# Second mixture weights loaded piece by piece into the tiles of first ones, with the dense part's first columns behind four first weights

## The chip, the cores and the metric

The kernel runs on one core of a Trainium2 chip. The time is the device time of one execution in microseconds (us). Before the change it is 387.07 us, the median of three runs (386.13 to 389.33).

## The reference, cut to what matters

Three stages follow each other, all in 32-bit floats except the last stage's weights, which are 64-bit floats in HBM.

1. Attention over 4 batches, 8 heads, 576 positions and 64 dimensions, with a local mask in four heads and a strided one in the other four. Its output, laid out as x of 2304 x 512, goes on.
2. A soft mixture of 8 experts. `logits = x @ phi` gives 32 slots, 4 for each expert. The softmax over tokens, transposed, times x gives the slot inputs. For each expert e, `h = max(slot_input[e] @ w1[e], 0)` and `slot_out[e] = h @ w2[e]`, where w1[e] is 512 x 1024 and w2[e] is 1024 x 512, 2 MB each. The softmax over slots times slot_out gives the new x.
3. A dense part: `h = x @ w_in` (512 x 2048), an ELU, and `g @ w_out` (2048 x 512) into the 2304 x 512 output.

## The kernel before, in words

Everything is emitted in one function. All DMAs are issued by SyncE (SP in the profile), in program order; its program lets eight transfers be under way, so a ninth waits until the one eight places ahead has landed. Each engine takes its instructions in order.

The attention runs over "units"; during them SP loads q, k and v and then the first mixture weights w1[0] to w1[7], as the table `LOADS` says, each into a "slot": a region of SBUF that q, k, v or a mask used before. `slot(i, name)` allocates a new tile in the region, and a new tile waits until every access to the tile before it in that region is done. `load_w(e, second, s)` loads weight w1[e] or w2[e] into slot s, in four transfers of 512 KB, w1 by halves of its rows and columns (line 459), w2 by two of its eight blocks of 128 rows (line 462). w2[0] and w2[1] go into the two halves `wb0` and `wb1` of the tile `xw`; w2[2], w2[3], w2[4], w2[5], w2[6] and w2[7] go into the slots of w1[0], w1[1], w1[2], w1[4], w1[6] and w1[7].

`emit_w1(a)` multiplies the slot inputs by w1 of experts 2a and 2a + 1 (line 638): for each of the four blocks of rows c, four matmuls side by side in four column groups of the array. `emit_h1T` transposes the result. `emit_w2(e)` (line 729) multiplies by the eight blocks of w2[e]; all eight experts add into one PSUM tile `yp` (called acc in the profile). Behind each pair of blocks of the last expert, and behind `emit_w2`, stand warm-up matmuls on the identity (`warm`, line 419; others, line 1088, stand where the dense part begins).

The dense weights come as 64-bit floats and are decoded: `dec_abs` on ScalarE (line 708), then `dec_1`, `dec_2`, `dec_3` on VectorE (lines 712, 716, 722). The first 256 columns of w_in (`WP`) are loaded by themselves, 1 MB in one transfer into slot 9, by `load_w64(0, 0, 9, (0, WP))` (line 697), ahead of w2[7]; the decoded values go over w2[0] in `wb0`. Behind the last expert SP loads pieces of w_out (line 703, 512 KB each) into `wb1` and the other 256 columns of the first part of w_in (line 697).

After the mixture `y_sb`, `sop` and `soT` turn yp into the operand of the dense part (lines 777 to 784). `soT` times the decoded w_in (`mps`, lines 860 to 877) gives a small matrix `M4`; from there the units of the dense part run: `hps` (line 951), the ELU (lines 955 to 971) and three output matmuls for each 128 tokens (lines 993 to 995). Their order is written by a planner with fixed costs and due times, which the change does not touch.

Of the kernel before, what the change touches and what calls it, by code (L numbers as in the profile page):

```python
# [10 lines left out]
I32 = mybir.dt.int32  # L11
# [8 lines left out]
def attn_moe_mlp(ctx, tc, q, k, v_l, v_s, phi, w1, w2, w_in, w_out, out):  # L20
    nc = tc.nc
    B, S, D = 4, q.shape[1] * q.shape[3] // 4, 64
    NT, DM = out.shape
    NE, _, FE = w1.shape
    w_in, w_out = w_in.bitcast(I32), w_out.bitcast(I32)
# [30 lines left out]
    WP, HP = 256, 2  # L56
# [14 lines left out]
    def region(tag, name):  # L71
        return slots.tile([128, SIZE[tag]], F32, tag=tag, name=name)

    def slot(i, name):
        if not isinstance(i, int):
            return i
        t = region(SLOT_AT[i], name)
        return t[:, 0:min(SLOT, t.shape[1])]
# [276 lines left out]
    with tc.manual_schedule():  # L355
# [7 lines left out]
        for b in range(B):  # L363
            sm_ = smask[32 * b:32 * b + 32, 0, :]
            nc.gpsimd.affine_select(
                out=sm_, in_=sm_, compare_op=ALU.is_ge, fill=NEG, base=0,
# [3 lines left out]
        for e in range(2):  # L370
            nc.vector.memset(qk_t[2][1][:, e, 0:576], 0.0)
        nc.vector.tensor_copy(
            out=smask16.rearrange("p (a b) -> p a b", b=MR), in_=smask.to_broadcast([128, 16, MR])
# [14 lines left out]
        for b in range(B):  # L388
            lm = lmask[32 * b:32 * b + 32]
            nc.gpsimd.affine_select(  # L390
                out=lm[:, 0:32], in_=lm[:, 0:32], compare_op=ALU.is_ge, fill=NEG, base=0,
# [3 lines left out]
                out=lm[:, 32:64], in_=lm[:, 32:64], compare_op=ALU.is_ge, fill=NEG, base=-1,  # L395
# [29 lines left out]
        for x in (576, 1152):  # L425
            for e in range(2):
                w = x // 576 * 576
                nc.scalar.activation(
                    out=qk_t[2][1][:, e, x:x + w], in_=zero.to_broadcast([128, w]), func=AF.Copy,
                )  # L430
        for b in range(B):
            nc.scalar.activation(
                out=e0[32 * b:32 * b + 32].rearrange("p (g x) -> p g x", x=32),
                in_=ident[0:32, 0:32].unsqueeze(1).to_broadcast([32, B, 32]), func=AF.Copy,
# [10 lines left out]
            load_k(3, c, c + 2)  # L445
            load_v_str(3, c // 2)

        wsl = {}

        def load_w(e, second, s, part=None):  # L450
            if (e, second) not in wsl:
                t = slot(s, f"w{e}_{second}")[:, 0:4096]
                wsl[e, second] = t.rearrange("p (c x) -> p c x", c=8 if second else 4)
            t = wsl[e, second]
            src = (w2 if second else w1)[e].rearrange("(c p) x -> p c x", p=128)
            if not second:
                for c in (0, 2):
                    for x in (0, 512):
                        nc.sync.dma_start(out=t[:, c:c + 2, x:x + 512], in_=src[:, c:c + 2, x:x + 512])
                return  # L460
            for c in range(0, 8, 2) if part is None else range(part, part + 4, 2):
                nc.sync.dma_start(out=t[:, c:c + 2], in_=src[:, c:c + 2])
# [103 lines left out]
        emit_dt(0)  # L566
        emit_PV(nu - 1, s_ps)
        load_w(7, 0, 1)
        emit_L(*pend_L.pop())
        emit_m(1)  # L570
# [37 lines left out]
        for t in range(3):  # L608
            nc.vector.tensor_scalar(
                out=e1[:, t], in0=e0[:, 0:NS], scalar1=rd, scalar2=wt[:, t:t + 1], op0=ALU.mult, op1=ALU.mult  # L610
# [19 lines left out]
        for t in (misc.tile([128, 1024], F32, tag="pst", name="h1T"), small("xt", 768, "h1T_b", 1), small("s", 256, "h1T_c", 3)):  # L630
            nc.gpsimd.memset(t, 0.0)
            t = t.rearrange("p (e c s) -> p e c s", c=8, s=NS)
# [53 lines left out]
        w64 = {}  # L686

        def load_w64(kind, i, s, part=None):
            if (kind, i) not in w64:
                t = slot(s, f"w64_{kind}_{i}")[:, 0:4096]  # L690
                w64[kind, i] = t.rearrange("p (c x a) -> p c x a", c=4, a=2).bitcast(I32)
            t = w64[kind, i].rearrange("p c x a -> p c (x a)")
            if kind == 0:
                src = w_in[:, 1024 * i:1024 * i + 1024].rearrange("(c p) f -> p c f", p=128)
                if part is not None:
                    t, src = t[:, :, 2 * part[0]:2 * part[1]], src[:, :, 2 * part[0]:2 * part[1]]
                nc.sync.dma_start(out=t, in_=src)
            else:
                src = w_out[512 * i:512 * i + 512, :].rearrange("(c p) x -> p c x", p=128)
                if part is None:  # L700
                    nc.sync.dma_start(out=t, in_=src)
                else:
                    nc.sync.dma_start(out=t[:, part], in_=src[:, part])
# [3 lines left out]
        def dec_abs(src, dst):  # L707
            nc.scalar.activation(out=dst, in_=src[:, :, 1].bitcast(F32), func=AF.Abs, scale=ESC)  # L708
# [24 lines left out]
                if e == NE - 1 and c in (1, 3, 5):  # L733
                    warm(W6)

        load_w64(0, 0, 9, (0, WP))
        load_w(7, 1, 1)
        pers = slot(6, "pers")
        dec = wb0.rearrange("p (i x) -> p i x", x=512)
# [3 lines left out]
        for i0 in range(0, NSET, 3):  # L743
            ps = ps_t.tile([128, 3, 128], F32, tag="t", name="ctps")
            for j in range(3):
                nc.tensor.transpose(ps[:, j, :], c4[:, i0 + j].rearrange("p a x -> p (a x)"), ident)
            nc.scalar.activation(
                out=cT[:, :, 32 * i0:32 * i0 + 96].rearrange("p b (j x) -> p j b x", x=32),
                in_=ps.rearrange("p j (b x) -> p j b x", b=B), func=AF.Copy,
# [2 lines left out]
            emit_w2(e)  # L752
            warm(W4)
        for c in range(4):
            dec_abs(w64[0, 0][:, c, 0:WP], dec[:, c, 0:WP])
        for c in range(4):
            for d_ in (dec_1, dec_2, dec_3):
                d_(w64[0, 0][:, c, 0:WP], dec[:, c, 0:WP])
        warm(W5)
        emit_w2(NE - 1)  # L760
        loads, due = {}, -1.35
# [250 lines left out]
        for si, gi, s, f0, f1, y, T in ev_n:  # L1012
# [18 lines left out]
            x = node("V" if f0 else "A", 0.6 if f0 else 0.48, deps, key, f_ev, ("ob", rel) if f1 == NF else None)  # L1031
            o_rel[k].append(x)
            last[j] = x
            if f1 == NF:
                rel.append(node("S", 0.73, [x], key, lambda j=j, ob=ob: nc.sync.dma_start(
                    out=out[128 * j:128 * j + 128, :], in_=ob["t"]
# [25 lines left out]
        while len(order) < len(nodes):  # L1062
            best = (1e8,)
            for e in free:
                c = [(start_of(n), nodes[n][3], n) for n in ready[e]]
                if c:
                    lim = min(c)[0] + EPS
                    x = min((key, t, n) for t, key, n in c if t <= lim)
                    best = min(best, (x[1], x[2], e))
            t, n, e = best  # L1070
# [69 lines left out]
```

## Time and profile before

| what | us |
|---|---|
| median of three runs | 387.07 |
| the profiled execution's own time | 386.45 |
| its span, first to last instruction | 384.7 |
| TensorE (PE) busy | 346.8 (90%) |
| VectorE (DVE) busy | 260.0 (68%) |
| ScalarE (ACT) busy | 234.2 (61%) |
| GpSimd (POOL) busy | 33.6 (9%) |
| moved by DMA | 71.63 MB |

The page gives busy shares over the whole span, the chain of work that ended last (each instruction followed back to what released it), and groups of instructions by line. The trace behind it can be asked for a stretch: the instructions of an engine in order, the busy time and the transfer rate by windows, what one line waited for, and how long its transfers took from issue to landing.

### The profile page before, as it was taken

The page shows a single profiled execution, that of the slowest core. Times are in us where ns is not written, and L with a number is a line of the kernel's source. Part 1 is how long each engine was busy: PE and PEld are TensorE (multiplying, and loading weights), DVE is VectorE, ACT ScalarE, POOL GpSimd, SP SyncE. Part 2 cuts the span into 40 slices and gives each one's busy share as a digit, 9 for nine tenths or more (in the row PEclk, how much of TensorE's full clock was granted, in tenths as well). Part 3 has the DMA queues.
Part 4 walks back from the last instruction along what each step waited for, and adds up shares of the span by engine and source line. Part 5 has one row for each costly group of instructions (what it writes and reads, how often), then busy time and mean ns, then how long its engine had stood idle before and what let it go on. Part 6 is the DMA issues. An engine that isn't in the chain of part 4 may idle for free.

```text
span 384.7 us, 8119 instructions
## 1 busy us (share of the span) xinstructions
PE 346.8 (90%) x3299; PEld 251.5 (65%) x3299; DVE 260.0 (68%) x537; ACT 234.2 (61%) x463; POOL 33.6 (9%) x67
## 2 busy tenths in 40 slices
PE   6457789786989968999999999999999999999995
PEld 4346566564424312778778868888877888888884
DVE  6566859677450005988989999999864756477641
ACT  6396765243332102899999868767666665666660
POOL 8403681000010000000000000000000000000000
PEclk9597999899999998999999999999999999999999
DMA  7999999968989999953600050500000011032201
GB/s 206 392 388 387 390 321 328 365 227 306 388 306 391 386 388 355 412 197 153 219 2 0 1 220 18 200 3 0 0 2 0 0 53 58 0 111 110 109 2 55
DMA packets 32773, 71.63 MB, mean 186 GB/s; under 512 B 2144, under 2 KB 2272, under 8 KB 32736
## 3 DMA queue, kind: packets, MB, share of 16 engines
q1 hardware_dynamic: 32736, 71.12, 50.5%
q8 instruction: 26, 0.43, 0.5%
q14 instruction: 11, 0.09, 0.1%
HBM read 66.39 MB, written 4.72 MB: 185 GB/s over the span
## 4 chain that ended last, share of the span: by engine, by line
PE 70%; DMA 18%; DVE 6%; ACT 2%; issue 2%; SPq 1%; DVEq 0%; ACTq 0%
PE ops L993 17%; PE ops L994 17%; PE ops L995 17%; DMA w<-in_moe_w_dram 8%; PE hps L951 4%; DMA kA<-in_k_dram 3%; DMA v<-in_v_l_dram 3%; DMA q<-in_q_dram 2%; DMA v<-in_v_s_dram 2%; PE s_ps L203 2%; PE xtps L337 2%; PE acc L729 1%; PE lo L295 1%; PE wps L1088 1%; PE mps L860 1%
## 5 line engine op out<-in xcount | busy, mean ns | idle before, releaser
L961 DVE SCALAR_TENSOR_TENSOR g<-hps,g 128x512 f32<-128x512 f32 (+1 forms) x80 | 50.7, 635 | 19.5 <-ACT g L958 19.4
L955 ACT ACTIVATE g<-hps 128x512 f32<-128x512 f32 (+1 forms) x80 | 44.3, 553 | 21.2 <-PE hps L951 19.8
L958 ACT ACTIVATE g<-g 128x512 f32<-128x512 f32 (+1 forms) x80 | 46.9, 586 | 1.4
L995 PE MATMUL ops<-wh,glo 128*128 128x512 f32 x86 | 33.5, 390 | 0.0
L995 PE MATMUL ops<-w,glo 128*128 128x512 f32 x86 | 33.5, 389 | 0.0
L967 ACT ACTIVATE ghi<-g 128x512 fp32r<-128x512 f32 (+1 forms) x40 | 23.5, 588 | 14.3 <-DVE g L961 12.9
L967 ACT ACTIVATE rings<-g 128x512 fp32r<-128x512 f32 (+1 forms) x40 | 23.4, 586 | 12.4 <-DVE g L961 10.3
L951 PE MATMUL hps<-pers 128*128 128x512 f32 (+1 forms) x80 | 29.4, 373 | 0.0
L993 PE MATMUL ops<-wh,ghi 128*128 128x512 f32 x72 | 28.9, 401 | 0.0
L993 PE MATMUL ops<-wh,rings 128*128 128x512 f32 x72 | 28.8, 400 | 0.0
L993 PE MATMUL ops<-w,ghi 128*128 128x512 f32 x72 | 28.5, 395 | 0.0
L712 DVE TENSOR_SCALAR xw<-xw 128x512 int32<-128x512 int32 (+1 forms) x36 | 13.8, 392 | 21.4 <-ACT xw L708 21.3
L994 PE MATMUL ops<-wl,ghi 128*128 128x512 f32 x72 | 28.1, 390 | 0.0
L994 PE MATMUL ops<-w,rings 128*128 128x512 f32 x72 | 28.1, 390 | 0.0
L993 PE MATMUL ops<-w,rings 128*128 128x512 f32 x72 | 28.1, 390 | 0.0
L994 PE MATMUL ops<-w,ghi 128*128 128x512 f32 x72 | 28.1, 390 | 0.0
L994 PE MATMUL ops<-wl,rings 128*128 128x512 f32 x72 | 28.0, 390 | 0.0
L708 ACT ACTIVATE xw<-w 128x512 f32<-128x512 f32 (+1 forms) x24 | 13.4, 588 | 17.4 <-DMA w<-in_moe_w_in_dram 17.4
L995 PE MATMUL ops<-wh,rings 128*128 128x512 f32 x58 | 22.6, 390 | 0.0
L995 PE MATMUL ops<-w,rings 128*128 128x512 f32 x58 | 22.6, 389 | 0.0
L512 POOL COPY v<-v 32x1152 f32<-32x1152 f32 (+2 forms) x20 | 19.2, 961 | 25.9 <-DMA v<-in_v_l_dram 25.1
L228 DVE TENSOR_REDUCE mx<-s_ps 128x6 f32<-128x384 f32 (+1 forms) x20 | 10.1, 506 | 15.0 <-PE s_ps L217 8.8
(184 smaller groups left out, 723.6 us busy)
## 6 DMA issues: line engine op xcount, KB each, us to landing
w<-in_moe_w_dram SPq DMA_DIRECT2D x56, 512.0 KB, 9.3
w<-in_moe_w_in_dram SPq DMA_DIRECT2D x3, 2048.0 KB, 8.8
out_dram<-ob SPq DMA_DIRECT2D x18, 256.0 KB, 2.0
v<-in_v_s_dram SPq DMA_DIRECT2D x8, 512.0 KB, 8.7
xw<-in_moe_w_dram SPq DMA_DIRECT2D x8, 512.0 KB, 9.1
xw<-in_moe_w_out_dram SPq DMA_DIRECT2D x2, 2048.0 KB, 7.7
q<-in_q_dram SPq DMA_DIRECT2D x7, 576.0 KB, 9.2
kB<-in_k_dram SPq DMA_DIRECT2D x8, 288.0 KB, 8.8
```

The costliest lines, as they stand in the source:

```text
L228: ops_.append(lambda: nc.vector.reduce_max(out=mx[:, 0:w, 0], in_=sc, axis=AX.X))
L512: nc.gpsimd.tensor_copy(out=o, in_=i)
L708: nc.scalar.activation(out=dst, in_=src[:, :, 1].bitcast(F32), func=AF.Abs, scale=ESC)
L712: nc.vector.tensor_scalar(out=d, in0=d, scalar1=3, scalar2=None, op0=ALU.logical_shift_left)
L951: nc.tensor.matmul(t["ps"], M4[:, 128 * f:128 * f + 128], cTf[:, t0:t0 + n], start=True, stop=True)
L955: nc.scalar.activation(out=t["g"], in_=t["ps"], func=AF.Exp)
L958: nc.scalar.activation(out=t["g"], in_=t["g"], func=AF.Relu, scale=-1.0, bias=1.0)
L961: nc.vector.scalar_tensor_tensor(out=t["g"], in0=t["ps"], scalar=0.0, in1=t["g"], op0=ALU.max, op1=ALU.subtract)
L967: nc.scalar.activation(out=t["hi"], in_=t["g"], func=AF.Copy)
L993: nc.tensor.matmul(o, t["hi"][:, c], hi, start=(f == f0), stop=False)
L994: nc.tensor.matmul(o, t["hi"][:, c], lo, start=False, stop=False)
L995: nc.tensor.matmul(o, t["lo"][:, c], hi, start=False, stop=(f == f1 - 1))
```

## The change

A tile that a first weight was loaded into is kept in `w_tiles` under its slot, and the second weight of that slot is written into the same tile instead of a new one. A transfer into a tile then waits for the accesses to the part that it overwrites, and no longer for those to the whole tile. Block c of w1 (1024 columns of the tile) lies where the blocks 2c and 2c + 1 of w2, one transfer, are written.

The first 256 columns of w_in are no longer one transfer into slot 9 ahead of w2[7]. They are four transfers of 128 rows (256 KB each), one behind each of w1[3], w1[4], w1[6] and w1[7], into the last 512 words of the tiles of slots 9, 5, 7 and 1, which the weights do not use. The decode reads them from there. `load_w64` still loads the other 256 columns into slot 9, now into a new tile.

```diff
-        wsl = {}
+        wsl, w_tiles, w64h = {}, {}, []
 
         def load_w(e, second, s, part=None):
             if (e, second) not in wsl:
-                t = slot(s, f"w{e}_{second}")[:, 0:4096]
+
+                if not isinstance(s, int):
+                    t = s
+                elif second:
+                    t = w_tiles[s]
+                else:
+                    t = w_tiles[s] = slot(s, f"w{e}")
+                t = t[:, 0:4096]
                 wsl[e, second] = t.rearrange("p (c x) -> p c x", c=8 if second else 4)
...
                         nc.sync.dma_start(out=t[:, c:c + 2, x:x + 512], in_=src[:, c:c + 2, x:x + 512])
+                if s in (9, 5, 7, 1):
+
+                    c = len(w64h)
+                    h = w_tiles[s][:, 4096:4096 + 2 * WP]
+                    nc.sync.dma_start(out=h.bitcast(I32), in_=w_in[128 * c:128 * c + 128, 0:2 * WP])
+                    w64h.append(h.rearrange("p (x a) -> p x a", a=2).bitcast(I32))
                 return
...
-        load_w64(0, 0, 9, (0, WP))
         load_w(7, 1, 1)
...
         for c in range(4):
-            dec_abs(w64[0, 0][:, c, 0:WP], dec[:, c, 0:WP])
+            dec_abs(w64h[c], dec[:, c, 0:WP])
         for c in range(4):
             for d_ in (dec_1, dec_2, dec_3):
-                d_(w64[0, 0][:, c, 0:WP], dec[:, c, 0:WP])
+                d_(w64h[c], dec[:, c, 0:WP])
```

On SP's queue, the first weights and what follows them stand like this before (w_0_915 is w1[2], w_0_1694 is w1[7], xw takes w2[0] and w2[1]):

```order
L459 DMA w_0_915<-in_moe_w_dram 128x2x512 x4
L459 DMA w_0_1195<-in_moe_w_dram 128x2x512 x4
L459 DMA w_0_1200<-in_moe_w_dram 128x2x512 x4
L459 DMA w_0_1336<-in_moe_w_dram 128x2x512 x4
L459 DMA w_0_1592<-in_moe_w_dram 128x2x512 x4
L459 DMA w_0_1694<-in_moe_w_dram 128x2x512 x4
L462 DMA xw<-in_moe_w_dram 128x2x512 x8
```

And now, with line numbers of the changed kernel:

```order
L466 DMA w_915<-in_moe_w_dram 128x2x512 x4
L466 DMA w_1195<-in_moe_w_dram 128x2x512 x4
L471 DMA w_1195<-in_moe_w_in_dram 128x512
L466 DMA w_1201<-in_moe_w_dram 128x2x512 x4
L471 DMA w_1201<-in_moe_w_in_dram 128x512
L466 DMA w_1338<-in_moe_w_dram 128x2x512 x4
L466 DMA w_1594<-in_moe_w_dram 128x2x512 x4
L471 DMA w_1594<-in_moe_w_in_dram 128x512
L466 DMA w_1697<-in_moe_w_dram 128x2x512 x4
L471 DMA w_1697<-in_moe_w_in_dram 128x512
L475 DMA xw<-in_moe_w_dram 128x2x512 x8
```

Four short transfers of w_in have come in, one behind each of w1[3], w1[4], w1[6] and w1[7].

The second weights w2[2] and w2[3] on SP's queue, with the semaphores that each transfer waits for (DMAHW: an earlier transfer; PE: matmuls), before:

```order
L462 DMA w_1_1863<-in_moe_w_dram 128x2x512 [waits DMAHW0_49,PE_49]
L462 DMA w_1_1863<-in_moe_w_dram 128x2x512 [waits DMAHW1_49]
L462 DMA w_1_1863<-in_moe_w_dram 128x2x512 [waits DMAHW2_49]
L462 DMA w_1_1863<-in_moe_w_dram 128x2x512 [waits DMAHW3_49]
L462 DMA w_1_1868<-in_moe_w_dram 128x2x512 [waits DMAHW4_49,PE_49]
```

And now:

```order
L475 DMA w_271<-in_moe_w_dram 128x2x512 [waits DMAHW4_49,PE_49]
L475 DMA w_271<-in_moe_w_dram 128x2x512 [waits DMAHW5_49,PE_49]
L475 DMA w_271<-in_moe_w_dram 128x2x512 [waits DMAHW6_49,PE_49]
L475 DMA w_271<-in_moe_w_dram 128x2x512 [waits DMAHW7_49,PE_49]
L475 DMA w_910<-in_moe_w_dram 128x2x512 [waits DMAHW0_49]
```

One wait for matmuls at the first piece has become one wait at each piece. The other second weights read alike.

The end of SP's mixture loads, before (w_1_1958 is w2[6], w_1_1972 is w2[7], w_0_0_1970 the tile of w_in in slot 9):

```order
L462 DMA w_1_1958<-in_moe_w_dram 128x2x512 x4
L697 DMA w_0_0_1970<-in_moe_w_in_dram 128x4x512
L462 DMA w_1_1972<-in_moe_w_dram 128x2x512 x4
L703 DMA xw<-in_moe_w_out_dram 128x1024 x2
L697 DMA w_0_0_1970<-in_moe_w_in_dram 128x4x512
```

And now:

```order
L475 DMA w_1594<-in_moe_w_dram 128x2x512 x4
L475 DMA w_1697<-in_moe_w_dram 128x2x512 x4
L716 DMA xw<-in_moe_w_out_dram 128x1024 x2
L710 DMA w_0_0_2103<-in_moe_w_in_dram 128x4x512
```

The 1 MB transfer between w2[6] and w2[7] is gone. The orders on TensorE, VectorE and ScalarE hold the same instructions in the same sequence as before.

## Rows read from the trace of the kernel before

**Rows 1.** Page, the chain that ended last: shares of the span by line.

```profile
PE ops L993 17%; PE ops L994 17%; PE ops L995 17%; DMA w<-in_moe_w_dram 8%; PE hps L951 4%; DMA kA<-in_k_dram 3%; DMA v<-in_v_l_dram 3%; DMA q<-in_q_dram 2%; DMA v<-in_v_s_dram 2%; PE s_ps L203 2%; PE xtps L337 2%; PE acc L729 1%; PE lo L295 1%; PE wps L1088 1%; PE mps L860 1%
```

**Rows 2.** Chain from 144 to 162 us: start us, us, what.

```profile
133.22 12.14 DMA w<-in_moe_w_dram
145.50 1.92 PE acc L729 x4
147.42 0.54 PE wps L419 x2
147.97 1.45 PE acc L729 x4
149.41 0.33 PE wps L419 x2
149.74 0.98 PE acc L729 x4
...
152.02 0.76 PE wps L419 x6
...
160.39 0.37 PE hps L951
```

**Rows 3.** Transfers of single issues (issues with first and last start; then issue to landing).

```profile
L697 SPq DMA_DIRECT2D w<-in_moe_w_in_dram x1: 671/671/671, 131.8 to 131.8; - x1
DMA to landing us min/median/max: 12.2/12.2/12.2
L462 SPq DMA_DIRECT2D w<-in_moe_w_dram x1: 471/471/471, 137.6 to 137.6; - x1
DMA to landing us min/median/max: 11.8/11.8/11.8
L462 SPq DMA_DIRECT2D w<-in_moe_w_dram x1: 368/368/368, 109.9 to 109.9; - x1
DMA to landing us min/median/max: 4.1/4.1/4.1
L136 SPq DMA_DIRECT2D kA<-in_k_dram x4: 601/604/613, 31.6 to 36.0; - x4
DMA to landing us min/median/max: 8.3/9.4/10.5
```

**Rows 4.** Windows: length, busy us of PE, PEld, DVE, ACT, POOL; PEclk, DMA share, GB/s.

```profile
86.00:88.00 2.00, 1.93 (x71) 1.14 (x63) 1.88 (x6) 0.43 (x1) 0.00 (x0) 1.00 0.08 18
90.00:92.00 2.00, 0.94 (x55) 0.51 (x39) 1.83 (x9) 0.59 (x3) 0.00 (x0) 1.00 0.95 336
110.00:112.00 2.00, 2.00 (x24) 0.65 (x20) 1.19 (x3) 0.68 (x1) 0.00 (x0) 1.00 0.71 180
112.00:114.00 2.00, 1.31 (x16) 0.13 (x4) 0.76 (x1) 1.88 (x4) 0.00 (x0) 1.00 0.80 282
114.00:116.00 2.00, 1.98 (x20) 0.91 (x24) 0.29 (x2) 0.46 (x1) 0.00 (x0) 1.00 0.91 328
137.00:139.00 2.00, 1.40 (x6) 0.29 (x8) 0.00 (x0) 0.00 (x0) 0.00 (x0) 1.00 1.06 391
145.50:147.50 2.00, 2.00 (x5) 0.32 (x6) 1.90 (x6) 0.01 (x1) 0.00 (x0) 0.50 1.05 388
```

**Rows 5.** What SP waited for, 103 to 112 us: us, times, longest.

```profile
SPq L462 <- PE s_ps L638: 6.5, 1, 6.5
```

**Rows 6.** Instructions in order: start us, us, what, count, idle time before and its end.

```profile
106.24 7.07 PE L638 MATMUL s_ps<-w,siT 128*32 128x512 f32 x64 [0.46 <-DVE siT L627]
...
141.33 1.05 PE L729 MATMUL acc<-w,h1T_b 128*32 128x512 f32 x4 [0.27 <-DMA w<-in_moe_w_dram]
...
144.12 1.39 ACT L708 ACTIVATE xw<-w 128x256 f32<-128x256 f32 x4 [17.44 <-DMA w<-in_moe_w_in_dram]
...
152.41 0.66 ACT L708 ACTIVATE xw<-xw 128x512 f32<-128x512 f32 x1
154.59 0.45 ACT L867 ACTIVATE mp<-mps 128x128 f32<-128x128 f32 x2 [1.52 <-PE mps L860]
```

## The prediction

> **What bounds the kernel now.** I read the page's chain first [rows 1]. The three output lines of the dense part hold 51% of the span, and the transfers of the mixture weights 8%, the largest share of any wait. So the dense part is TensorE's own work, and what can move its start is the transfer of weights ahead of it. The chain around that start [rows 2] shows the place: a piece of w2[7], issued at 133.22, lands 12.14 us later at 145.36. From 145.50 on every link is TensorE: the last expert, its warm-up matmuls, the way to `soT`, and the first dense units at 160.4. If w2[7] lands earlier, all of that starts earlier. The third view is the transfers themselves [rows 3]. The 1 MB of w_in's first columns is issued at 131.8 and lands at 144.0, between the last piece of w2[6], whose landing releases TensorE at 141.33 [rows 6], and the first of w2[7]; the last piece of w2[7] is issued at 137.6 and lands at 149.4. The fourth is the windows [rows 4]: with SP's eight transfers under way the stream runs at 391 GB/s, but at 110 to 116 us it falls to 180, 282 and 328, and at 86 to 88 us it stands nearly still at 18. For the first hole the row on SP says why: it waited 6.5 us for the matmuls of line 638 before it could issue w2[2] [rows 5].
>
> So the mixture's end is set by bytes in the stream and by a hole in it, and the dense part by when the stream is done.
>
> **The change, part by part.**
>
> *The 1 MB between w2[6] and w2[7] goes.* It held the stream from about 141.3 to 144.0, and 1.05 MB at 391 GB/s is 2.7 us: w2[7] lands 2.7 us earlier.
>
> *Piecewise reuse.* The 64 matmuls from 106.24 take 7.07 us [rows 6], so the 32 of the first two experts take some 3.6, and a quarter of these, block c = 0, some 0.9. The first piece of w2[2] can be issued at about 107.2 instead of 109.9, the others follow 0.9 us apart. A transfer on an idle queue took 4.1 us from issue to landing [rows 3], and the stream falls below 300 GB/s only after 110: the new pieces are behind the old ones before it runs dry. The hole was 211, 109 and 63 GB/s below 391 for 2 us each, 766 KB or 1.95 us. I take all of it; the lower bound is the next item, because what is added fills the hole otherwise.
>
> *Four transfers of 256 KB are added*, 0.67 us each at 391 GB/s. The two behind w1[3] and w1[4] go out before the standstill at 86 to 88 us and move what follows to the right only until there, where there is room for them: cost nothing. If that cover were gone they would cost 1.35 us. The two behind w1[6] and w1[7] fall into the stream that begins at 88 us and has no other hole left: 1.35 us, or a little less since that stream starts at 336 GB/s with the engines 95% busy. I take 1.1; the ends are 0.6 and 1.35. Nothing waits for w1 or w2[0] there: `emit_w1` begins at 106.24, and the second weights are used behind it.
>
> A short transfer might cost more than its bytes. Four of 288 KB, issued from 31.6 to 36.0, landed 10.5 and 8.3 us later for the first and the last [rows 3], that is from 42.1 to 44.3, 0.73 us apart, which is their bytes at 395 GB/s: inside a full stream the rows show no price by the piece. The Trainium skill, "DMA: Bandwidth & Descriptors", section "Bandwidth", has a rule that speaks against the change: batch transfers to 1 MiB or more for 75% of the peak. Its section on the anatomy of one DMA gives about 2.0 us fixed per transfer for another issue path; by it the two transfers in the full stream would cost an estimated 4 us more, and little would be left of the gain. I go by the row.
>
> Transfers together: -2.7 - 1.95 + 1.1 = -3.55, so the last piece of w2[7] lands at 145.9 instead of 149.4.
>
> *TensorE's clock at the last expert.* The first groups of the last expert took 1.92 and 1.45 us and a warm-up pair 0.54, the next 0.98 and 0.33 [rows 2]. The granted clock was 0.50 of full there, 1.2 GHz, and 1.00, 2.4 GHz, at 137 to 139 us [rows 4]; before it fell TensorE stood idle for the 3 us of the 1 MB. With idle times of 0.3 us between groups [rows 6] it stayed at 1.00. After the change w2[7] follows w2[6] a piece later, so the idle time there is some 0.3 us too and the clock should stay. The last expert then ends 0.14 + 0.98 us after its last piece lands, at 147.0; before it ended at 152.02, 2.6 us after. That is 1.5 us more. Bounds: 0 if the clock falls all the same, 1.5.
>
> *The decode of the first columns moves up.* Four `dec_abs` on ScalarE, from 144.12 on, and twelve steps on VectorE behind them now run as soon as expert 0 has been read. ScalarE stood idle for 17.44 us before them [rows 6], that is from 126.7, and next in both queues is `y_sb`, which needs the last expert's end at 152.02: cost nothing, gain nothing. SP no longer waits for the decode before it loads the other 256 columns; that is no gain either while the dense part needs them late.
>
> *What is late next.* Behind w2[7] comes the first piece of w_out, 1.35 us later, at about 147.25. ScalarE's decode of it stood at 152.41 [rows 6] and moves to 147.4: just in time, and 1.52 us of idle time behind it [rows 6] covers a small delay.
>
> From there on every engine's order is as before, and TensorE's work of the dense part is not shortened or lengthened: 5.0 us earlier at 147 should be 5.0 us earlier at the end.
>
> **Sum.** -3.55 - 1.5 = -5.05 against the profiled execution's 386.45: 381.4. The median of the runs shown is 0.6 above that execution, so I forecast 381.9, 1.3% faster. By the ends of the terms this forecast lies between 380.5 and 383.3.
>
> **The rivals.**
>
> 1. *The earlier landing counts, the clock does not.* TensorE falls to 0.50 in the last expert again, or the piece of w_out is late by what the clock gave. Either takes the 1.5 us back: 383.4. For it: the pieces arrive just as fast as TensorE uses them up, one slip of a transfer is enough. Against it: 137 to 142 us at the same pace was granted 1.00. Chance 0.19.
> 2. *The change does not do what it says at the first hole*: the pieces wait as long as the whole tile did. Then the hole stays, the two late short transfers lie in it, and the gain is 2.7 + 1.5 = 4.2: 382.8. Against it: each piece of w2[2] has a wait for matmuls of its own. Chance 0.05.
> 3. *Each short transfer costs a fixed time in the stream.* From the rows: 4.1 us alone less 1.34 us of bytes is 2.8. Two of them in the full stream would add 5.6, the last piece would land at 151.5, and with the warm clock the last expert would end at 152.6: 387.7, no change. The rule of "DMA: Bandwidth & Descriptors" in the Trainium skill leads here; four transfers 0.73 us apart stand against it. Chance 0.04.
> 4. *Slower: the half clock moves into the way to the dense part.* Now the last two experts both run at the pace of the transfers, some 11 us of groups with idle time between them instead of 5.5. If that lowered the grant from 147 on, the chain that ran from 152.02 to 160.39 would take 8.4 us longer: 390, slower than before. It decides from 60% of that stretch at 0.50, where 5.05 us are used up. For it: the clock did fall in this place once. Against it: it fell after 3 us of nothing, not at this pace. Chance 0.03.
>
> **Numbers.** My forecast has 0.69. About 1% (3.9 us) is what a measurement of this kernel can tell from no change; the line is 383.2. Of the forecast's chance I put 0.62 below it; rival 1 lies on it and gives 0.06, rival 2 gives 0.04: faster 0.72. Same: 0.24 (the rest of the forecast, most of rival 1, rival 3). Slower: 0.04. The range goes from 380.4, the best end of the terms, to 384.9, past rivals 1 and 2 with 1.5 us for the spread of the runs; rivals 3 and 4 and a little of each end are left out.
>
> **What would show it.** In the changed kernel's profile: no window below 380 GB/s from 96 us until w2[7] is in; SP's wait for line 651 (638 before) shorter than 4 us; w2[7]'s last piece landing at 145 to 146.5; the idle time before the last expert below 1 us, its groups at 0.98 us and the granted clock at 1.00; the decode of the first columns done by 133; the first `hps` about 5 us earlier than before and the same difference at the last output. I am wrong if the stream between 88 and 112 us is slowed by more than 1.4 us, if the last expert's groups still take 1.5 us or more, or if the first dense unit moves by less than w2[7] does.

## The result and the profile after

The changed kernel takes 383.6 us (median, 383.3 to 386.05) against 388.2 us for the kernel before (386.13 to 389.7): 0.988 of it [0.983, 0.993]. Compared twice more, in later rounds on two chips, it came to 383.94 against 388.06 (0.991 [0.987, 0.994]) and 384.75 against 389.07 (0.989 [0.985, 0.992]). So the gain is 4.1 to 4.6 us; the forecast was 5.05 and 381.9. Of the 1.7 us between 381.9 and 383.6, some 1.2 are the starting point, since the forecast counts from 387.0 and the kernel before came to 388.2 here; some 0.5 are the gain. By its number alone the result also fits rival 1 of the prediction (383.4), and the gain fits rival 2's 4.2; the traces tell them apart.

The one execution that was profiled hides this. Its time is 386.05, at the upper end of the changed kernel's times, and the profiled one of before, 386.45, lay at the lower end of its own; the spans are 384.3 and 384.7. So the two traces can't be compared from the start of the span. They can be compared from a point behind which all of the change but its first two short transfers works: the issue of w1[6], the first load behind the standstill. It stands at 86.38 us before and at 91.49 after, since TensorE reached the attention's unit that frees the slot 5.1 us later. From there, times worked out from the traces:

| from the issue of w1[6], us | before | after | difference | predicted |
|---|---|---|---|---|
| to the last landing of w2[7] | 63.04 | 59.54 | -3.50 | -3.55 |
| to the end of the last expert | 65.64 | 60.63 | -5.01 | -5.05 |
| to the first `hps` | 69.82 | 64.81 | -5.01 | -5.05 |

The match to 0.05 us is partly luck: before's first trace has a longer stream than two of the three others of its kind (below).

The chain that ended last in the changed kernel, from 136 to 156 us, start and us, answers to [rows 2]:

```profile
136.14 10.82 DMA w<-in_moe_w_dram
146.96 0.14 issue
147.10 1.05 PE acc L742 x4
148.15 0.33 PE wps L419 x2
148.48 0.98 PE acc L742 x4
149.46 0.33 PE wps L419 x2
149.78 0.99 PE acc L742 x4
150.78 0.33 PE wps L419 x2
151.10 1.02 PE acc L742 x4
152.12 0.76 PE wps L419 x6
```

The first piece of w2[7] still releases the last expert, but its groups now take 1.05, 0.98, 0.99 and 1.02 us where two of the four took 1.92 and 1.45. The last expert ends at 152.12, 1.09 us after the last landing (151.03); before it was 2.60. TensorE in order shows why, with its idle time before and what ended it in brackets ([rows 6] before):

```profile
144.30 1.05 PE L742 MATMUL acc<-w,h1T_b 128*32 128x512 f32 x4 [0.30 <-DMA w<-in_moe_w_dram]
145.66 1.05 PE L742 MATMUL acc<-w,h1T_b 128*32 128x512 f32 x4 [0.31 <-DMA w<-in_moe_w_dram]
147.10 1.05 PE L742 MATMUL acc<-w,h1T_c 128*32 128x512 f32 x4 [0.39 <-DMA w<-in_moe_w_dram]
```

The idle time ahead of the last expert is 0.39 us instead of 3.12, and the windows have a granted clock of 1.00 there instead of 0.50. The same view (columns as in [rows 4]) shows the place of the hole:

```profile
110.00:112.00 2.00, 1.54 (x15) 0.70 (x18) 1.55 (x3) 0.00 (x0) 1.50 (x3) 0.90 1.05 386
112.00:114.00 2.00, 2.00 (x12) 0.44 (x8) 1.22 (x3) 0.68 (x1) 0.00 (x0) 0.50 1.06 389
114.00:116.00 2.00, 2.00 (x20) 0.56 (x16) 1.68 (x4) 0.18 (x1) 0.00 (x0) 0.75 1.05 386
116.00:118.00 2.00, 2.00 (x24) 0.57 (x20) 0.76 (x1) 1.86 (x4) 0.00 (x0) 1.00 1.05 386
147.00:149.00 2.00, 1.90 (x10) 0.43 (x10) 0.00 (x0) 0.00 (x0) 0.00 (x0) 1.00 1.06 390
```

386 to 389 GB/s where [rows 4] had 180 to 328, and 387 from 118 to 126 us. The granted clock fell to 0.50 at 111.6 us, behind the start of `emit_w1` at 110.76, and the matmuls that free the slots took longer for it: SP's waits for them, 103 to 118 us, are 5.7 us in four pieces, where [rows 5] had one of 6.5.

```profile
SPq L475 <- PE s_ps L651: 5.7, 4, 2.8
```

It cost nothing: the first piece of w2[2] was issued at 111.93, 6.6 us ahead of the last landing of w2[1] at 118.57. Before, these stood at 109.91 and 112.06, 2.15 us apart, less than the 4.1 us that this first piece took to land [rows 3]. (The prediction calls it a transfer on an idle queue; two pieces of w2[1] were still under way when it was issued. The first piece of w1[6], issued into the standing stream, took 4.2.)

How much the stream moved from the issue of w1[6] to the last landing of w2[7], before and then after:

```profile
DMA packets 11616, 22.87 MB, mean 363 GB/s; under 512 B 671, under 2 KB 671, under 8 KB 11611
```

```profile
DMA packets 11340, 22.21 MB, mean 373 GB/s; under 512 B 683, under 2 KB 683, under 8 KB 11335
```

This row splits the 3.50 us in two: 0.66 MB less at 373 GB/s is 1.8 us, and 22.87 MB at 363 instead of 373 GB/s is 1.7 us. The bytes include what transfers behind w2[7] moved meanwhile; the change itself takes 0.52 MB out of the stretch, which is 1.4 us at that rate.

The rest of the prediction's list: the decode of the first columns, and ScalarE at the start of the dense part.

```profile
132.59 1.47 ACT L721 ACTIVATE xw<-w 128x256 f32<-128x256 f32 x4 [0.46 <-PE acc L742]
152.23 0.39 ACT L789 ACTIVATE y_sb<-acc 128x256 f32<-128x256 f32 x1 [18.17 <-PE acc L742]
152.51 0.66 ACT L721 ACTIVATE xw<-xw 128x512 f32<-128x512 f32 x1
154.69 0.45 ACT L879 ACTIVATE mp<-mps 128x128 f32<-128x128 f32 x2 [1.51 <-PE mps L872]
```

The decode runs at 132.59, 14.5 us ahead of the last expert, and waits for expert 0's matmuls only. The decode of w_out stands straight behind `y_sb`, and the 1.51 us of idle time behind it are those of [rows 6]: the piece of w_out was in time. The first `hps` starts at 156.20 before and at 156.30 now; the 160.39 that the prediction takes from [rows 2] for the first dense unit is a later `hps`.

### The profile page after: what moved, and what is told of

It is laid out like the page before. It is cut to its first block, busy times and chain, and to the rows that moved or that the text cites. A ratio compares the mean times of both kernels' runs of the same rounds, so it can differ in the third digit from the quotient of the medians.

```text
span 384.3 us, 8143 instructions
## 1 busy us (share of the span) xinstructions
PE 348.8 (91%) x3299; PEld 253.5 (66%) x3299; DVE 259.8 (68%) x537; ACT 234.4 (61%) x463; POOL 33.7 (9%) x67
## 4 chain that ended last, share of the span: by engine, by line
PE 71%; DMA 18%; DVE 6%; issue 2%; ACT 2%; SPq 0%; DVEq 0%; ACTq 0%
PE ops L1005 17%; PE ops L1006 17%; PE ops L1007 17%; DMA w<-in_moe_w_dram 8%; PE hps L963 4%; DMA kA<-in_k_dram 3%; DMA v<-in_v_l_dram 3%; DMA q<-in_q_dram 2%; DMA v<-in_v_s_dram 2%; PE s_ps L203 2%; PE lo L295 2%; PE xtps L337 1%; PE s_ps L651 1%; PE wps L1100 1%; PE mps L872 1%
## 5 line engine op out<-in xcount | busy, mean ns | idle before, releaser
L967 ACT ACTIVATE g<-hps 128x512 f32<-128x512 f32 (+1 forms) x80 | 44.2, 553 | 21.2 <-PE hps L963 19.8
L983 DVE TENSOR_TENSOR glo<-g,rings 128x512 fp32r<-128x512 f32 (+1 forms) x24 | 15.2, 634 | 7.2 <-ACT rings L979 4.3
L983 DVE TENSOR_TENSOR glo<-g,ghi 128x512 fp32r<-128x512 f32 (+1 forms) x24 | 15.2, 633 | 5.0 <-ACT ghi L979 2.4
```

Source lines behind the costliest of these rows:

```text
L967: nc.scalar.activation(out=t["g"], in_=t["ps"], func=AF.Exp)
L983: nc.vector.tensor_tensor(out=t["lo"], in0=t["g"], in1=t["hi"].bitcast(F32), op=ALU.subtract)
```

## The experiments

Four explanations were on the table. **A**: the landing of w2[7] sets the mixture's end, and the half clock adds 1.5 us behind it; that is the prediction's. **B**: the two short transfers behind w1[3] and w1[4] hold up the attention and eat part of the gain, as the 5.1 us between the two traces could suggest. **C**: nearly all of the gain is the clock. And, beside these, whether a short transfer has a price of its own. "Stream" below is always from the issue of w1[6] to the last landing of w2[7], "the hole" is the dip of its rate at 110 to 116 us, and "the slot inputs are ready" is the time at which the operand of `emit_w1` (`siT`) stands.

### The piecewise reuse alone

```diff
...
-                t = slot(s, f"w{e}_{second}")[:, 0:4096]
+                if not isinstance(s, int):
+                    t = s
+                elif second:
+                    t = w_tiles[s]
+                else:
+                    t = w_tiles[s] = slot(s, f"w{e}")
+                t = t[:, 0:4096]
```

> The second weights go piece by piece into the tiles of the first ones, but the first 256 columns of w_in are again one transfer of 1 MB ahead of w2[7]. Theory A (the end is set by the landing of w2[7] and by TensorE's clock behind it): the hole at 110 to 116 us goes, w2[7] lands 1.95 us earlier than before, the 3 us of idle time ahead of the last expert and its half clock stay; about 2 us faster than before (ratio 0.995). Rival B (the two early short transfers delay the end of the attention, and that took back 2 to 4 us of the change): without them nothing is taken back, also about 2 us faster, and the siT operand stands near 106 us as before. Rival C (nearly all of the change's gain is the clock of the last expert): no gain, ratio 1.000, since the idle time stays.

387.03 us against 389.11, 0.995 [0.991, 0.998]. The stream is 61.64 us, 1.4 below before's first trace, and moved at 373 GB/s:

```profile
DMA packets 11657, 23.00 MB, mean 373 GB/s; under 512 B 679, under 2 KB 679, under 8 KB 11652
```

But the 1 MB still stands ahead of w2[7], TensorE idles for 3.12 us, and the chain has three slow groups instead of two:

```profile
145.78 1.92 PE acc L736 x4
147.70 0.54 PE wps L419 x2
148.24 1.85 PE acc L736 x4
150.09 0.54 PE wps L419 x2
150.63 1.28 PE acc L736 x4
```

The last expert ends 3.51 us after the last landing. The medians, 2.1 us apart, are what A says. The one trace shows less: 1.4 us of stream are gained and 0.9 behind the landing are lost, so the last expert ends 65.15 us behind the issue of w1[6], 0.5 less than in before's first trace. How much of the hole this kernel wins in a usual execution isn't shown.

### The columns moved, without the piecewise reuse

The whole change, but w2[2] is issued last piece first, so that its first transfer waits for the last block of w1[0], as the whole tile did. The later second weights still go piece by piece.

```diff
-            for c in range(0, 8, 2) if part is None else range(part, part + 4, 2):
+            for c in (6, 4, 2, 0) if e == 2 else range(0, 8, 2) if part is None else range(part, part + 4, 2):
```

> The whole change, but the four pieces of w2[2] are loaded in the opposite order, so that the first of them waits for the last block of w1[0] and all four go out as late as before the change. Theory A: the hole at 110 to 116 us is back, the two late short transfers fall into it, and 2.7 us of the removed 1 MB and 1.5 us of clock remain; 4.2 us faster than before, at most 1 us slower than the whole change. Rival B: as much slower or faster than the whole change as its attention happens to end, with the siT operand near 110 us. Rival C: as fast as the whole change.

384.29 us against 389.11, 0.988 [0.983, 0.994]: as much as the whole change, within the interval. The stream is 59.27 us and as full:

```profile
110.00:112.00 2.00, 2.00 (x24) 0.58 (x20) 1.68 (x4) 0.18 (x1) 0.00 (x0) 1.00 1.05 386
112.00:114.00 2.00, 1.83 (x20) 0.33 (x12) 0.76 (x1) 1.86 (x4) 0.00 (x0) 1.00 1.03 377
114.00:116.00 2.00, 1.45 (x12) 0.71 (x16) 0.29 (x2) 0.98 (x3) 0.00 (x0) 1.00 1.05 391
```

The first piece of w2[2] was issued at 110.43, as late as before (3.7 us after the slot inputs are ready at 106.71, in both), but the last of w2[1] landed only at 114.27, since two short transfers had gone ahead of it: 3.84 us. Two transfers are 1.35 us of bytes; without them the lead would have been an estimated 2.5. So the bytes that were put ahead of the hole seem to have filled it. That is argued from one execution: before's second trace had a lead of 3.76 us without any short transfer, and still a small dip (278, 373 and 344 GB/s at 110 to 116 us). In this execution the two parts of the change look like two remedies for one hole, and their gains don't add up; the pair with two late transfers, below, has a case in which they do.

### The clock alone

Before, with 16 warm-up matmuls ahead of the last expert.

```diff
-    W0, W2, W3, W4, W5 = 8, (0, 0, 0, 0, 0), 3, 0, 0
+    W0, W2, W3, W4, W5 = 8, (0, 0, 0, 0, 0), 3, 0, 8
```

> The kernel before, with 16 warm-up matmuls ahead of the last expert, where TensorE stood idle for 3 us (they need 2.6 us). Theory A: the granted clock stays at 1.00 in the last expert, its groups take 0.98 us, it ends 1.1 to 1.3 us after the last piece lands instead of 2.6; 1.4 us faster than before (ratio 0.996). Rival B says nothing else. Rival C: 4 us faster, as much as the whole change.

387.08 us against 389.11, 0.996 [0.993, 0.999], which is 2.0 us (0.5 to 2.9), though w2[7] lands as late as before and later. TensorE from 145 us on:

```profile
145.08 1.05 PE L729 MATMUL acc<-w,h1T_b 128*32 128x512 f32 x4 [0.30 <-DMA w<-in_moe_w_dram]
146.07 1.92 PE L419 MATMUL wps<-ident 128*128 128x256 bf16 x16
149.23 1.05 PE L729 MATMUL acc<-w,h1T_c 128*32 128x512 f32 x4 [1.24 <-DMA w<-in_moe_w_dram]
```

```profile
147.20:149.20 2.00, 0.79 (x8) 0.46 (x6) 0.81 (x3) 1.34 (x4) 0.00 (x0) 1.00 1.05 387
```

The idle time is cut to 1.24 us, the clock stays at 1.00, and the last expert ends 1.10 us after the last landing instead of 2.60. That is the 1.5 us of the prediction. The change gains 4.1 to 4.6, and C's 4 us lie outside the interval: C is dead.

### The 1 MB put back ahead of w2[7], as other bytes

The whole change with two pieces of w_out, 1 MB together, loaded ahead of w2[7] instead of behind it.

```diff
-        load_w(7, 1, 1)
...
+        for c in range(2):
+            load_w64(1, 0, wb1, c)
+        load_w(7, 1, 1)
...
-            load_w64(1, 0, wb1, c)
+            if c >= 2:
+                load_w64(1, 0, wb1, c)
```

> The whole change, with the first two pieces of w_out (1 MB together) loaded ahead of w2[7] and not behind it: the same bytes, and 1 MB between w2[6] and w2[7] as in the kernel before. Theory A: w2[7] lands 2.7 us later after w2[6], TensorE idles for 3 us ahead of the last expert, the grant falls to 0.50 and the end comes 2.6 us after the landing or later: 4.2 us slower than the whole change in the same rounds, and at most 1 us faster than the kernel before. Theory C (nearly all of the gain is the clock, where the transfers land matters little): 1.5 us slower than the whole change. A third (what counts is that the 1 MB of w_in is decoded early): no slower than the whole change.

388.19 us (385.09 to 390.33) against 383.94 for the whole change in the same rounds and 388.06 for before: 1.000 [0.997, 1.004] of before. The whole gain is gone with one move of 1 MB. The stream has no hole (375 GB/s), but is 62.04 us long, 2.5 more than with the change; and behind it:

```profile
142.95 1.05 PE L742 MATMUL acc<-w,h1T_b 128*32 128x512 f32 x4 [0.29 <-DMA w<-in_moe_w_dram]
146.97 1.92 PE L742 MATMUL acc<-w,h1T_c 128*32 128x512 f32 x4 [2.96 <-DMA w<-in_moe_w_dram]
```

2.96 us of idle time, 1.92 us for the first group, and the end 2.41 us after the landing instead of 1.10. 2.5 + 1.3 is 3.8 of the 4.25 us measured between the medians. That the decode of w_in still runs early is of no help, which bears out its price of nothing.

### All four short transfers late

```diff
-                if s in (9, 5, 7, 1):
-
-                    c = len(w64h)
+                for c, s in enumerate((9, 5, 7, 1) if e == 7 else ()):
```

> The whole change, but all four short transfers stand behind w1[7] instead of one behind each of four first weights. Theory A: 1 MB in the full stream instead of 0.5 MB, w2[7] lands 1.35 us later than in the whole change; 1.3 us slower than it, 3.3 us faster than before. Rival B: up to 85 us everything is as before the change, the attention is not delayed, and this kernel is 1 to 3 us faster than the whole change. Rival C: as fast as the whole change.

385.42 us against 389.11, 0.991 [0.988, 0.994], 1.1 us above the kernel with the columns moved alone, of the same rounds. The four land 0.65 to 0.68 us apart (102.87, then 103.55, 104.20, 104.88 and 105.56), which is their bytes, and the stream runs at 373 GB/s. But it is 62.46 us long, where 0.52 MB more than the whole change would make 60.9. The row of bytes has the difference: 23.30 MB were moved, 1.09 more than in the whole change and not 0.52. The place is one landing: a piece came in 2.87 us behind the one before it (115.05, then 117.92) and not 1.35, while the windows around it kept 384 to 389 GB/s. So bytes of other transfers moved in that time; why is open.

### Two short transfers more, in the kernel before and in the piecewise one

Read by nobody, behind w1[6] and w1[7]. The edit to the kernel before, where `full` is the whole tile; the piecewise one has `w_tiles[s]` in its place:

```diff
-                t = slot(s, f"w{e}_{second}")[:, 0:4096]
+                full = slot(s, f"w{e}_{second}")
+                t = full[:, 0:4096]
...
+                if e in (6, 7):
+                    nc.sync.dma_start(out=full[:, 4096:4096 + 2 * WP].bitcast(I32), in_=w_in[128 * (e % 4):128 * (e % 4) + 128, 0:2 * WP])
```

> The kernel before, with two short transfers (256 KB each, read by nobody) behind w1[6] and w1[7]. Theory A as the prediction summed it (the terms stand side by side): the stream from the issue of w1[6] to the last landing of w2[7] grows from 63.0 by 1.1 to 1.35 us. Theory A with the hole as a buffer: the two fill a part of the hole at 110 to 116 us, and the stream is 63.0 to 63.3 us as before. A fixed price for each short transfer: 66 us or more.

> The kernel with the piecewise reuse alone, and the same two short transfers behind w1[6] and w1[7]. Its stream without them was 61.6 us. Terms side by side: 62.7 to 63.0. With the hole as a buffer (most of the hole is filled already by the pieces, only what was left of it takes the transfers): 62.0 to 62.7. A fixed price: 64.5 or more.

One execution each, 388.85 and 384.93 us, and the pair that tells most about the hole. In both the slot inputs are ready at 107.2 to 107.3 us, and in both the clock falls to 0.50 just there, so that the first 64 matmuls of `emit_w1` take 8.77 and 8.55 us instead of 7.07. The windows from 110 us, first of the kernel before with the two transfers, then of the piecewise one:

```profile
110.00:112.00 2.00, 2.00 (x20) 0.53 (x16) 1.57 (x4) 0.29 (x1) 0.00 (x0) 0.77 1.05 386
112.00:114.00 2.00, 2.00 (x24) 0.65 (x20) 1.15 (x2) 1.44 (x3) 0.00 (x0) 1.00 0.72 243
114.00:116.00 2.00, 2.00 (x20) 0.39 (x12) 0.00 (x0) 1.10 (x2) 0.00 (x0) 1.00 0.78 261
116.00:118.00 2.00, 2.00 (x24) 0.87 (x24) 0.29 (x2) 0.60 (x1) 0.00 (x0) 1.00 0.96 268
```

```profile
110.00:112.00 2.00, 2.00 (x24) 0.53 (x20) 1.65 (x4) 0.21 (x1) 0.00 (x0) 0.92 1.05 387
112.00:114.00 2.00, 2.00 (x24) 0.53 (x20) 1.07 (x2) 1.52 (x3) 0.00 (x0) 1.00 1.06 389
114.00:116.00 2.00, 2.00 (x22) 0.54 (x15) 0.00 (x0) 1.07 (x3) 0.00 (x0) 1.00 1.05 383
116.00:118.00 2.00, 2.00 (x20) 0.73 (x22) 0.29 (x2) 0.54 (x1) 0.00 (x0) 1.00 1.05 386
```

The streams are 64.33 and 61.95 us. The two short transfers lie ahead of the hole in the first, as in the kernel with the columns alone, and yet 243, 261 and 268 GB/s remain: with `emit_w1` at half clock the whole tile comes free at 112.7, 2.27 us ahead of w2[1]'s last landing. The pieces come free from 109.25 on, 5.56 us ahead, and there is no hole. The first number is that of "side by side", but not for that reason, so it decides nothing between the first two expectations. The second, 0.3 us above the piecewise kernel without the two transfers, lies just below the lowest of all three. A fixed price is excluded by both.

The second trace also holds an exception that the prediction's rule of the clock doesn't have:

```profile
146.04 1.05 PE L738 MATMUL acc<-w,h1T_c 128*32 128x512 f32 x4 [3.11 <-DMA w<-in_moe_w_dram]
```

TensorE stood idle for 3.11 us ahead of the last expert, as before the change, and yet the granted clock stayed at 1.00 and the last expert ended 1.10 us behind the landing. In the six other traces with 2.96 to 3.12 us of idle time there it fell to 0.50. What made the difference isn't shown. The 3.9 us between the two executions are then 2.4 of stream and 1.5 of clock, and only the first is the pieces' doing.

### Two short transfers early, in the kernel before

```diff
-                t = slot(s, f"w{e}_{second}")[:, 0:4096]
+                full = slot(s, f"w{e}_{second}")
+                t = full[:, 0:4096]
...
+                if e in (3, 4):
+                    nc.sync.dma_start(out=full[:, 4096:4096 + 2 * WP].bitcast(I32), in_=w_in[128 * (e % 4):128 * (e % 4) + 128, 0:2 * WP])
```

> The kernel before, with nothing changed but two more short transfers (256 KB each, of w_in, read by nobody) behind w1[3] and w1[4], where the change puts its first two. Theory A: they lie ahead of the standstill of the stream and cost nothing: siT is ready between 106 and 110 us as in all runs, the stream from the issue of w1[6] to the last landing of w2[7] is 63.0 us as before, the time is within 0.3% of the kernel before. Theory B (these two slow the attention, and take a part of the gain that the whole change should have): siT at 109 us or later and the time 0.5 to 1% above the kernel before.

388.34 us against 388.1, 1.000 [0.997, 1.004]: they cost nothing that these rounds can tell, and at most 0.4%. The profiled execution, 389.99, was slow in the attention all the same: the slot inputs were ready at 110.86. Its stream is 61.72 us and the end 2.61 us behind the landing, as before. The time speaks against B; the one trace doesn't, which is why the early transfers were then moved (below).

### Before and the whole change once more, and the early transfers in the standstill

The first two have no edit. The third moves the first two short transfers behind w1[5], where SP then waits for the slot of w1[6] and the stream stands still:

```diff
-                if s in (9, 5, 7, 1):
+                for x in {5: (9, 5), 6: (7,), 7: (1,)}.get(e, ()):
 
                     c = len(w64h)
-                    h = w_tiles[s][:, 4096:4096 + 2 * WP]
+                    h = w_tiles[x][:, 4096:4096 + 2 * WP]
```

> The whole change once more, on the same chip and in the same rounds as the next kernels. Theory A (the landing of w2[7] sets the mixture's end, and the half clock in the last expert adds 1.5 us behind it): from siT's readiness to the end of the last expert 41.0 to 41.5 us, against 45.8 before; the last expert ends 1.1 us after w2[7] lands; the time is 4.4 to 5 us below the kernel before where both have the same attention, 0.987 to 0.989 of it. siT itself is ready anywhere between 106 and 111 us, as in all runs so far, since that is not the change's doing. Theory B (the short transfers behind w1[3] and w1[4] slow the attention): siT is ready at 110 us or later, as in the first trace of the change, 4 us behind a trace of the kernel before.

> The kernel before, profiled a second time. Theory A: from siT's readiness to the end of the last expert 45.5 to 46 us again, the idle time before the last expert 3.1 us, the end 2.6 us or more after the landing; siT is ready at a time that may differ by some us from the 106.2 us of the first trace, with the difference in stalls of TensorE that no wait explains. Theory B: siT is ready at 106 us again, within 0.5 us.

> The whole change with its first two short transfers behind w1[5], in the standstill of the stream ahead of w1[6], and no longer behind w1[3] and w1[4]. What is open: from the first issue of w1[3] to siT's readiness the seven traces without short transfers there took 41.7 to 42.9 us, the five with them 43.4, 43.7, 41.3, 43.3 and 46.0. Theory A (they are free behind w1[3] and w1[4]; the spread is that of TensorE's own stalls): the same time as the whole change within the interval, and the stretch anywhere between 41.3 and 46 us. Theory B, now as a smaller effect (two more transfers in the stream beside the attention hold it up by some 1 us): the stretch at 42.5 us as in the kernels without them, the time about 1 us below the whole change. Both: the stream from the issue of w1[6] to the last landing of w2[7] at 59.5 us, the last expert's end 1.1 us behind it.

> The whole change beside the kernel with its first two short transfers in the standstill, on the same chip. Theory A: w1[3] to siT between 41.3 and 46 us, stream 59.5 us, end 1.1 us behind the landing, 0.988 to 0.991 of the kernel before. Theory B: w1[3] to siT at 43.3 us or more for the third time.

The whole change: 383.94 (0.991 [0.987, 0.994]) and 384.75 us (0.989 [0.985, 0.992]); before again 387.5 against 388.06 (1.000); with the early two in the standstill 384.48 (0.988 [0.984, 0.992]), on the same chip as the 384.75. From the traces, us:

| kernel | w1[3] issued | slot inputs ready | between | stream | end after landing |
|---|---|---|---|---|---|
| before, first | 63.52 | 106.18 | 42.66 | 63.04 | 2.60 |
| before, again | 64.88 | 106.55 | 41.67 | 61.87 | 2.58 |
| before, two early | 64.90 | 110.86 | 45.96 | 61.72 | 2.61 |
| whole change, first | 67.32 | 110.71 | 43.39 | 59.54 | 1.09 |
| whole change, again | 65.49 | 109.19 | 43.70 | 59.56 | 1.10 |
| whole change, third | 65.15 | 109.31 | 44.16 | 59.80 | 1.09 |
| columns alone | 65.39 | 106.71 | 41.32 | 59.27 | 1.09 |
| early two in the standstill | 67.04 | 108.77 | 41.73 | 59.61 | 1.09 |

The last two columns are A's, in every row. In the first trace of the change the attention was already 3.8 us late when w1[3] was issued, ahead of any short transfer. Most of the 5.1 us between the two first traces therefore isn't the change's doing. What lies behind w1[3] was 41.7 to 42.9 us in the eight traces without early transfers. Of the six with them five lie above all of these, 43.3 (the 1 MB put back), 43.4 to 44.2 (the whole change) and 46.0; the sixth, the columns alone, has 41.3. By the medians the version that takes the early two out of that stretch is 0.3 us faster, well inside its interval. So B is dead as an effect of several us; as one of some 1 us it stays open, and the traces lean towards it.

## Why the prediction was right

- **The bytes**, -2.7 + 1.1 = -1.6: by the row of bytes 1.8 us (0.66 MB at 373 GB/s), of which 1.4 are the change's own 0.52 MB. Right in its mechanism and nearly in its size, and shown from the other side when the 1 MB was put back and 4.25 us were lost. Short transfers show no price besides their bytes in the rate: the streams with none, two and four of them late run at 373, 375 and 373 GB/s. Rival 3 is dead. The Trainium skill, "DMA: Bandwidth & Descriptors", section "Bandwidth", asks for transfers of 1 MiB or more for 75% of the peak. These rates don't bear that out as a price of 256 KB transfers in a full queue.
- **The hole**, -1.95: measured 1.7 us against before's first trace. Right there, but its size is not a constant of the kernel. The four traces that have before's order of loads with nothing added behind w1[5] (before's two, the two early transfers, the warm-ups) moved 363, 370, 369 and 356 GB/s and took 63.04, 61.87, 61.72 and 63.58 us, 62.55 on average; the one that I read lay above that. The rows of the other three:

```profile
DMA packets 11623, 22.90 MB, mean 370 GB/s; under 512 B 670, under 2 KB 670, under 8 KB 11618
DMA packets 11590, 22.76 MB, mean 369 GB/s; under 512 B 670, under 2 KB 670, under 8 KB 11585
DMA packets 11563, 22.67 MB, mean 356 GB/s; under 512 B 667, under 2 KB 667, under 8 KB 11558
```

What goes with the size is the lead, the time from the first issue of w2[2] to the last landing of w2[1]: in the five traces with 0.70, 2.15, 2.27, 2.50 and 3.76 us the stream ran at 356, 363, 364, 369 and 370 GB/s, in the nine with 3.84 us or more at 372 to 375.

Against the change's 59.63 (three traces) the 62.55 are 2.9 us, and with 1.5 for the clock 4.4: the 4.1 to 4.6 of the medians. Where the forecast's 5.05 was too much, it is this term. Nor is it simply added to the others: in the one trace with the columns alone there was no hole without the pieces, at full clock in `emit_w1`, and in the one pair at half clock the pieces closed a hole that two late transfers did not.
- **The clock**, -1.5: right, 1.09 us behind the landing for 2.60, and the same 1.5 by warm-ups alone. Rival 1 did not occur in any of the six traces with the columns moved and no 1 MB put back. But its size isn't a constant either: one of seven traces with 3 us of idle time kept the clock at 1.00. An execution of the kernel before that does so would gain nothing by this term.
- **The decode and w_out**, nothing: right. The decode was to be done by 133 and was done at 137.65, later by the attention's delay, still 9 us ahead of the last expert.
- **Rival 2** is excluded by SP's row, four waits instead of one, and not by the time, which its 4.2 us would fit. **Rival 4** did not come: 1.00 in the windows behind 147 us.
- **What the list had wrong** are its absolute times, and SP's wait: it was to be shorter than 4 us and came to 5.7, with the half clock in `emit_w1` (2.2 and 3.8 in the two repeats, at full clock). From 96 us on no window was to lie below 380 GB/s; 96 to 100 us had 326 and 356, since the stream began 5.1 us later, and none behind that did. The last landing was to be at 145 to 146.5 and the first `hps` 5 us earlier; they stand at 151.03 and 156.3, as late as before. Counted from the issue of w1[6] both are right to 0.05 us. I took the attention's end for a fixed point, and it is not.
- **Two of its sums** don't come out. 381.4 and 0.6 are 382.0 and not 381.9. And the terms' best ends (0.6 for the late transfers) give 381.5, where the forecast's band starts at 380.5 and the range at 380.4. Neither changes the account.

## What to carry to other kernels

Count a gain from the last event that both programs share, not from the start of the span: the two first traces differed by 5.1 us here, 3.8 of them ahead of anything that was changed. Whether a queue's stretch got shorter by bytes or by a hole is read in one row, megabytes and mean rate between two events. And a hole that hangs on when a buffer comes free has no fixed size here, nor had the clock behind an idle time; read both in more than one execution before they go into a sum. Finer release closed the hole in the one pair in which bytes that lay ahead of it did not.

## What was not expected of the hardware

The attention's end lies between 106.2 and 110.9 us in the fourteen traces, and between 106.7 and 110.7 in the five whose instructions are the same up to there (the change and its repeats, the columns alone, the 1 MB put back). On TensorE's chain of the changed kernel stands a link in which it waited for nothing that the profile shows:

```profile
77.74 0.81 PE xtps L337 x6
79.17 2.87 issue
82.46 0.83 PE ptps L275 x3
83.61 1.44 PE s_ps L203 x24
```

Such stalls, of 1 to 3.4 us each, begin at 61 to 67, 71 to 80 and 94 to 99 us, not all of them in every execution; the two of before's first trace that are over 1 us measure 1.16 and 1.84. During this one, at 80.9 us, the granted clock fell to 0.50: the 24 matmuls of line 203 then took 1.44 us, at 87.74 us 0.79. What TensorE waited for in them was not tested and stays open. The half clock wanders in the same way: in seven of the fourteen traces it fell in `emit_w1` or just ahead of it, whose first 32 matmuls then took 5.0 to 5.3 us and not 3.6, and in before's two it didn't.
